# Chunked attention, gated projection and a two-layer block on one core: the first block's order by hand, its transposes and right-hand sums moved

## The chip, the cores and the metric

The kernel runs on one core of a Trainium2 chip. The core has five engines that run at the same time and wait for each other by semaphores: TensorE (PE in the rows; its weight loads are PEld), VectorE (DVE), ScalarE (ACT), GpSimd (POOL) and SyncE (SP), which here only issues transfers. Each works off its own queue in order. The metric is the device time of one execution in microseconds (us); lower is better.

## The reference

Everything is float32 at the interface; the eight sequences of 576 rows and 512 columns make 4,608 rows.

```python
# 1. attention inside chunks of 64 rows, 8 heads of 64 columns
attn = softmax(q_c @ k_c.T / sqrt(64)); x = attn @ v_c          # heads side by side: 512 columns
# 2. gated projection
gate = sigmoid(causal depthwise convolution of x with 5 taps)
y = (gate * (x @ w_val)) @ w_out
# 3. two-layer block with normalised input and residual
yn = (y - mean(y)) / sqrt(var(y) + 1e-6) * g_ln
out = y + relu(yn @ w_ch1) @ w_ch2                              # 512 -> 2048 -> 512
```

The wide weights arrive as pairs of 32-bit words (64-bit floats), which the kernel decodes itself.

## The kernel before, in words

**Number format.** Every float32 matmul is written as three matmuls on a high and a low part: high by high, high by low, low by high. A high part is a rounding copy on ScalarE; the low part is the difference, made on VectorE or GpSimd (`high_low`, L409; `split`, L112).

**Decoding.** A weight tile of 128x512 arrives as raw words (`load_ff`, L141). `decode` (L104) is one ScalarE instruction (L107) and three on VectorE (L108, L109, L110); `split` then adds the high part on ScalarE (L115) and the low part on GpSimd (L116). The decoded first-layer tile is also stored to DRAM (L159) for later use. Of the 32 tiles (16 groups f, one of each layer) those of groups 0 to 3 are made early, those of groups 4 and up just before and during the first block.

**Stages.** Attention and the gated projection run first and leave y in DRAM, nine blocks of 512 rows. Then comes the third part in two forms. The *first block* (rows 0 to 511) is computed directly: for each group f of 128 hidden columns `ff1` (L378) makes 12 matmuls into a hidden tile (psh), ScalarE rectifies it into the high part hh (L387), VectorE makes the low part hl (L388), and `ff2` (L393) multiplies them by the second layer into four accumulators with 12 matmuls (L403). TensorE runs one ff1 ahead of ff2. Two psh buffers alternate.

The other eight blocks go in four passes s of two blocks each, in *paired products* (`ff_pair`, L514): for two groups of hidden columns at once, seven products of 6 matmuls (`prod`, L520) between sums of left-hand weight tiles (wc) and sums of right-hand row tiles (b11, b21, b22 and t1 to t4), accumulated into the two PSUM tiles zy and x; copies and additions (L540, L544) and rectifiers (L535, L536) recover the four hidden tiles h. The second layer of a pair (`ff2_tile`, L487) fills TensorE during the next pair, as the list `fill`.

Around the seam between the two forms stand: the normalisation of the 8 row tiles of pass 0, two at a time (`ln_rows`, L346: statistics L352, L353 and small corrections on VectorE, a square root and the scaling L366 on ScalarE, transposes L369 on TensorE, copies L371 on ScalarE into xt); the right-hand sums (`right_operands`, L453), made from xt by VectorE additions (L463) and high and low parts (L410, L411); the left-hand sums of pair p (`make_pair`, L421), made from stored decoded tiles that are loaded again (raws, L433, L434), with subtractions on VectorE (L435 to L438) and low parts on GpSimd (L411), then stored (L443) for the later passes. Their tiles form a ring; ring positions 0 to 3 use the same memory as the first-layer tiles of groups 0 to 3 and 8 to 11.

**What sets the order.** A scheduler of the framework orders each engine's instructions at build time by priority and by modelled times; on the chip the order is fixed. Inside `manual_schedule` an engine follows the order of the program instead. Before, that holds for TensorE up to unit 7 of attention and from the paired products on, not in the first block. Memory pools that are opened after others are closed (`s_1`, `s_0`) take over their place, and instructions that write there wait for the last reader.

## Time and profile before

| | |
|---|---|
| median of 3 runs | 1196.09 us (1195.82 to 1197.68) |
| the profiled execution | 1193.61 us, its span 1191.8 us |
| TensorE busy | 1114.5 us, 94% of the span; mean granted clock 0.977 |
| VectorE busy | 738.2 us, 62% |
| ScalarE busy | 527.4 us, 44% |
| GpSimd busy | 158.1 us, 13% |

All rows come from the one profiled execution, times counted from its span's start. Attention and the gated projection take the first 378 us. The first block's first hidden product starts at 378.6 us, its last accumulation ends at 493.5 us, and the paired products follow. A row of the timeline is one instruction, or several alike in a run (x12), with its start, its length and in brackets the time the engine was idle before it and who ended the wait. Instructions on TensorE overlap, so twelve that are 0.39 us long each can take 2.96 us in all.

### The profile page before, as it was taken

The numbers are of one execution on the slowest core, as the hardware profiler recorded it, in microseconds if no ns is written. First come the engines' busy times: TensorE is split into PE (matmuls) and PEld (weight loads), VectorE is DVE, ScalarE is ACT, GpSimd is POOL, SyncE is SP. The second block draws the span as 40 slices with busy tenths as digits, with TensorE's granted clock in tenths as the row PEclk, the third lists the DMA queues.
The fourth block names the chain that finished last, engine by engine and source line by source line (L and its number), as shares of the span: only waits on it lengthen the run. The fifth ranks groups of instructions, "written<-read, shape, count | busy, mean of one in ns | idle before, by whom it ended". The sixth has DMA issues, their size and how long they took to land.

```text
span 1191.8 us, 18298 instructions
## 1 busy us (share of the span) xinstructions
PE 1114.5 (94%) x7128; PEld 902.3 (76%) x7128; DVE 738.2 (62%) x1237; ACT 527.4 (44%) x972; POOL 158.1 (13%) x160
## 2 busy tenths in 40 slices
PE   7859999899999688789999999999999999999998
PEld 6747777777777566568888878888788887878876
DVE  6878899988894985644564753534835436442433
ACT  4557678676666564333443323332413424221221
POOL 2221133111211433322221000000000000000000
PEclk8979999999999999989999999999999999999999
DMA  7655676655113673233333353332532332622212
GB/s 182 172 114 131 166 190 182 176 148 131 45 63 126 213 248 119 98 133 124 142 124 106 126 194 105 106 124 89 198 120 89 124 106 98 223 86 89 89 36 79
DMA packets 168860, 155.37 MB, mean 130 GB/s; under 512 B 120622, under 2 KB 128838, under 8 KB 168774
## 3 DMA queue, kind: packets, MB, share of 16 engines
q1 hardware_dynamic: 163590, 144.76, 39.7%
q10 hardware_dynamic: 5184, 9.44, 2.1%
q8 instruction: 56, 0.92, 0.3%
q14 instruction: 30, 0.25, 0.1%
HBM read 116.41 MB, written 37.75 MB: 129 GB/s over the span
## 4 chain that ended last, share of the span: by engine, by line
PE 61%; DVE 26%; ACT 5%; issue 3%; SPq 2%; DMA 1%; POOL 1%; DVEq 0%; POOLq 0%; ACTq 0%
PE acc L501 14%; PE x L526 14%; PE psf L501 14%; PE zy L526 9%; DVE cg L281 8%; PE psv L295 3%; DVE da L109 2%; DVE pr L211 2%; DVE da L110 2%; PE pso L295 2%; DVE sm L208 2%; PE psh L295 2%; DVE ex L202 1%; PE pst L369 1%; DVE mx L199 1%
## 5 line engine op out<-in xcount | busy, mean ns | idle before, releaser
L544 DVE TENSOR_TENSOR c<-x,c 128x512 f32<-128x512 f32 x96 | 66.1, 689 | 231.5 <-ACT c L540 175.1
L501 PE MATMUL acc<-w,h 128*128 128x512 f32 x768 | 186.0, 391 | 0.0
L501 PE MATMUL psf<-w,h 128*128 128x512 f32 x768 | 186.0, 391 | 0.0
L501 PEld LDWEIGHTS acc<-w,h 128*128 128x128 f32 x768 | 144.2, 188 | 31.4
L501 PEld LDWEIGHTS psf<-w,h 128*128 128x128 f32 x768 | 144.2, 188 | 31.3
L526 PE MATMUL x<-t,wc 128*128 128x512 f32 x576 | 149.4, 395 | 4.6 <-DVE c L544 4.2
L540 ACT ACTIVATE c<-zy 128x512 f32<-128x512 f32 x96 | 57.9, 603 | 195.2 <-PE zy L526 195.2
L526 PEld LDWEIGHTS x<-t,wc 128*128 128x128 f32 x576 | 109.3, 190 | 29.6 <-DVE c L544 5.1
L535 ACT ACTIVATE h<-c 128x512 fp32r<-128x512 f32 x96 | 60.5, 631 | 135.8 <-DVE c L544 135.2
L281 DVE SCALAR_TENSOR_TENSOR cg<-xf,cw,cg 128x516 f32<-128x516 f32 (+1 forms) x176 | 116.3, 707 | 0.8 <-ACT cg L279 0.6
L506 DVE TENSOR_TENSOR yt<-psf,yt 128x512 f32<-128x512 f32 x128 | 88.0, 689 | 23.8 <-PE psf L501 19.7
L526 PE MATMUL zy<-b,wc 128*128 128x512 f32 x384 | 100.1, 397 | 0.0
L526 PEld LDWEIGHTS zy<-b,wc 128*128 128x128 f32 x384 | 72.1, 190 | 14.9
L536 DVE SCALAR_TENSOR_TENSOR h<-c,h 128x512 fp32r<-128x512 f32 x96 | 68.0, 709 | 13.1 <-ACT h L535 12.7
L269 POOL TENSOR_TENSOR xl<-xf,xh 128x512 fp32r<-128x512 f32 (+1 forms) x40 | 50.3, 1260 | 154.1 <-ACT xh L268 153.9
L295 PE MATMUL psv<-xh,vh 128*128 128x512 f32 x144 | 60.3, 419 | 7.1 <-DVE gv L309 6.1
L411 POOL TENSOR_TENSOR wc<-raws,wc 128x256 fp32r<-128x256 f32 x56 | 48.4, 885 | 132.5 <-ACT wc L410 132.4
L295 PE MATMUL pso<-oh,gh 128*128 128x512 f32 x144 | 60.1, 417 | 5.6 <-ACT gh L312 5.1
L295 PE MATMUL psv<-xl,vh 128*128 128x512 f32 x144 | 57.5, 399 | 0.9 <-POOL xl L269 0.9
L295 PE MATMUL pso<-oh,gl 128*128 128x512 f32 x144 | 56.9, 397 | 0.7 <-DVE gl L313 0.7
L295 PE MATMUL psv<-xh,vl 128*128 128x512 f32 x144 | 57.4, 398 | 0.0
L526 PE MATMUL zy<-t,wc 128*128 128x512 f32 x192 | 50.6, 399 | 7.0 <-ACT t L410 3.9
(114 smaller groups left out, 1777.7 us busy)
## 6 DMA issues: line engine op xcount, KB each, us to landing
wc<-wc SPq DMA_DIRECT2D x112, 512.0 KB, 3.2
raw<-in_moe_w_ch SPq DMA_DIRECT2D x32, 512.0 KB, 5.0
yr<-yd SPq DMA_DIRECT2D x48, 256.0 KB, 3.0
vr<-in_v SPq DMA_DIRECT2D x144, 64.0 KB, 2.6
yd<-y ACTq DMA_DIRECT2D x36, 256.0 KB, 2.5
kr<-in_k SPq DMA_DIRECT2D x64, 128.0 KB, 2.9
qr<-in_q SPq DMA_DIRECT2D x64, 128.0 KB, 3.0
out<-yt SPq DMA_DIRECT2D x20, 256.0 KB, 3.1
```

The costliest lines, as they stand in the source:

```text
L109: nc.vector.scalar_tensor_tensor(out=au, in0=hw, scalar=0x80000000, in1=au, op0=ALU.bitwise_and, op1=ALU.bitwise_or)
L269: nc.gpsimd.tensor_tensor(out=xl[j][:, :, lo:hi], in0=src, in1=xh[j][:, :, lo:hi], op=ALU.subtract)
L281: nc.vector.scalar_tensor_tensor(out=o, in0=x[:, f, i + lo:i + hi], scalar=cw[:, i * CT + f:i * CT + f + 1], in1=o, op0=ALU.mult, op1=ALU.add,
L295: nc.tensor.matmul(out=ps, lhsT=lt, rhs=rh, start=(i == 0), stop=(i == n - 1))
L411: eng.tensor_tensor(out=lo, in0=a, in1=hi, op=ALU.subtract)
L501: nc.tensor.matmul(out=ps, lhsT=lt, rhs=rh, start=(g == 0 and k == 0 and (first or half)), stop=(g == 1 and k == 2 and (last or half)),)
L506: nc.vector.tensor_tensor(out=yt[i], in0=ps, in1=yt[i], op=ALU.add)
L526: nc.tensor.matmul(out=ps, lhsT=lt, rhs=rh, start=(start and c == 0 and i == 0), stop=(c == 1 and i == 2), skip_group_check=True)
L535: nc.scalar.activation(out=t[:, 0, :], in_=src, func=ACTF.Relu)
L536: nc.vector.scalar_tensor_tensor(out=t[:, 1, :], in0=src, scalar=0.0, in1=t[:, 0, :], op0=ALU.max, op1=ALU.subtract)
L540: nc.scalar.activation(out=t, in_=zy, func=ACTF.Copy)
L544: nc.vector.tensor_tensor(out=t, in0=x, in1=t, op=ALU.add)
```

## The change

In the first block TensorE's order is now written by hand, from the first hidden product on: `manual_schedule` opens before the block instead of behind it. `ln_rows` is split: it only normalises, and `turn_rows` does the transposes and copies. The rows of pair i are loaded ahead, normalised at high priority two groups before they are transposed, and transposed behind the hidden products 3, 5, 7 and 9. The rectifier and the low part of the hidden tile get high priority too. Weights are decoded at the end of each turn of the loop and loaded one group later. The first-layer tiles of groups 8 to 11 move to a pool of their own, and those of groups 12 to 15 take the ring's memory. After group 12's turn the pools are changed over and the right-hand sums are issued, so that they fall into the last three groups. The last second product (ff2 of group 15) and the remaining pools become the one filler of the first pair, behind its first two products, and that pair's first rectifier comes after the filler.

```diff
--- before.py
+++ after.py
@@ -151,7 +151,7 @@
     def split_ff(f, pool):
         r1, r2 = wraw.pop(f)
         g, m = divmod(f, NFA)
-        if g % 2 == 0:
+        if g in (0, 3):
             t = wA.tile([P, 2, DM], F32R, tag=f"s{NFA + m}", name="w0")
         else:
             t = p2[f"w{g}"].tile([P, 2, DM], F32R, tag=f"w{m}", name="w0")
@@ -343,7 +343,7 @@
         nc.sync.dma_start(out=t, in_=rows(s, i)[0])
         return t
 
-    def ln_rows(ys, i):
+    def ln_rows(ys):
 
         n = len(ys)
         mv = p2["b"].tile([P, n, 2], F32, tag="mv", name="mv")
@@ -364,6 +364,11 @@
         nc.vector.scalar_tensor_tensor(out=w, in0=mv[:, :, 0], scalar=-1.0, in1=r, op0=ALU.mult, op1=ALU.mult)
         for t, y in enumerate(ys):
             nc.scalar.activation(out=y, in_=y, func=ACTF.Identity, scale=r[:, t:t + 1], bias=w[:, t:t + 1])
+        return ys
+
+    def turn_rows(ys, i):
+
+        for t, y in enumerate(ys):
             ps = ps_t.tile([P, CT, P], F32, tag="t", name="pst")
             for c in range(CT):
                 nc.tensor.transpose(out=ps[:, c, :], in_=y[:, c * P:(c + 1) * P], identity=ident)
@@ -384,8 +389,9 @@
         chain(ps, ops)
         a = p2["h"].tile([P, BLK], F32R, tag="hh", name="hh")
         b = p2["h"].tile([P, BLK], F32R, tag="hl", name="hl")
-        nc.scalar.activation(out=a, in_=ps, func=ACTF.Relu)
-        nc.vector.scalar_tensor_tensor(out=b, in0=ps, scalar=0.0, in1=a, op0=ALU.max, op1=ALU.subtract)
+        with tc.high_priority():
+            nc.scalar.activation(out=a, in_=ps, func=ACTF.Relu)
+            nc.vector.scalar_tensor_tensor(out=b, in0=ps, scalar=0.0, in1=a, op0=ALU.max, op1=ALU.subtract)
         hh[j, f] = (a, b)
 
     acc = {}
@@ -516,6 +522,7 @@
         zy = ps_d.tile([P, BLK], F32, tag="d", name="zy")
         x = ps_d.tile([P, BLK], F32, tag="d", name="x")
         h = {}
+        first = s == 0 and p == 0
 
         def prod(ps, k, nm, start):
             g = (s * NPR + p) * 7 + k
@@ -551,8 +558,11 @@
         c = copy()
         prod(x, 1, "b11", True)
         add(c)
-        relu((0, 0), c)
+        if not first:
+            relu((0, 0), c)
         run(0, 3)
+        if first:
+            relu((0, 0), c)
         prod(zy, 2, "t1", True)
         d = copy()
         prod(x, 3, "t2", False)
@@ -638,7 +648,7 @@
             yt0 = p2["0"].tile([P, HB, DM], F32, name="yt0")
             y0 = y_dram[0].rearrange("(t p) d -> p t d", p=P)
             nc.sync.dma_start(out=yt0, in_=y0)
-            ln_rows([yt0[:, i, :] for i in range(HB)], 0)
+            turn_rows(ln_rows([yt0[:, i, :] for i in range(HB)]), 0)
             nc.sync.dma_start(out=yt0, in_=y0)
             for i in range(0, HB, 2):
                 ts = slice(i * P, (i + 2) * P)
@@ -676,8 +686,10 @@
     p2["w"] = ctx.enter_context(tc.tile_pool(name="wB", bufs=1, reuse_waits="tile"))
     s_1 = ExitStack()
     p2["w1"] = s_1.enter_context(tc.tile_pool(name="w1p", bufs=1, reuse_waits="tile"))
+    p2["w2"] = s_1.enter_context(tc.tile_pool(name="w2p", bufs=1, reuse_waits="tile"))
     stg2 = s_1.enter_context(tc.tile_pool(name="stg2", bufs=2, reuse_waits="tile"))
-    p2["w3"] = s_1.enter_context(tc.tile_pool(name="w3p", bufs=1, reuse_waits="tile"))
+    order = ExitStack()
+    order.enter_context(tc.manual_schedule(engines={mybir.EngineType.PE}))
 
     def next_ff(f):
         if NFA <= f < NF:
@@ -685,33 +697,43 @@
             load_ff(f, pool)
             split_ff(f, pool)
 
-    def rows_of(s, i, t):
+    def pair_rows(i):
+        t = stg2.tile([P, 2, DM], F32, tag="y", name="yr")
         for k in range(2):
-            nc.sync.dma_start(out=t[:, k, :], in_=rows(s, i + k)[0])
+            nc.sync.dma_start(out=t[:, k, :], in_=rows(0, i + k)[0])
         return [t[:, k, :] for k in range(2)]
 
     next_ff(NFA)
     next_ff(NFA + 1)
+    ys = {0: pair_rows(0)}
     for f in range(NF):
         ff1(0, f)
+        if f in (3, 5, 7, 9):
+            turn_rows(ys.pop(f - 3), f - 3)
         if f > 0:
             ff2(0, f - 1)
-        next_ff(f + NFA + 2)
-        if f in (3, 5, 7, 9):
-            ln_rows(rows_of(0, f - 3, stg2.tile([P, 2, DM], F32, tag="y", name="yr")), f - 3)
-    ff2(0, NF - 1)
-    s_1.close()
-    p2["xb"] = ctx.enter_context(tc.tile_pool(name="xb", bufs=1, reuse_waits="tile"))
-    s_0.close()
-    p2["hr"] = ctx.enter_context(tc.tile_pool(name="p2r", bufs=5, side="right", reuse_waits="tile"))
-    p2["wx"] = ctx.enter_context(tc.tile_pool(name="p2w", bufs=1, side="right", reuse_waits="tile"))
-    p2["c"] = ctx.enter_context(tc.tile_pool(name="pc", bufs=2, reuse_waits="tile"))
-    p2["yt"] = ctx.enter_context(tc.tile_pool(name="pyt", bufs=2, reuse_waits="tile"))
+        if f in (1, 3, 5, 7):
+            if f < 7:
+                ys[f + 1] = pair_rows(f + 1)
+            with tc.high_priority():
+                ln_rows(ys[f - 1])
+        if f > 0:
+            next_ff(f + NFA + 1)
+        if f == NF - 4:
+            s_1.close()
+            p2["xb"] = ctx.enter_context(tc.tile_pool(name="xb", bufs=1, reuse_waits="tile"))
+            p2["c"] = ctx.enter_context(tc.tile_pool(name="pc", bufs=2, reuse_waits="tile"))
+            right_operands()
     make_pair(0)
-    right_operands()
-    order = ExitStack()
-    order.enter_context(tc.manual_schedule(engines={mybir.EngineType.PE}))
-    fill = []
+
+    def open_rest():
+        ff2(0, NF - 1)
+        s_0.close()
+        p2["hr"] = ctx.enter_context(tc.tile_pool(name="p2r", bufs=5, side="right", reuse_waits="tile"))
+        p2["wx"] = ctx.enter_context(tc.tile_pool(name="p2w", bufs=1, side="right", reuse_waits="tile"))
+        p2["yt"] = ctx.enter_context(tc.tile_pool(name="pyt", bufs=2, reuse_waits="tile"))
+
+    fill = [open_rest]
     for s in range(NS):
         for p in range(NPR):
             fill = ff_pair(s, p, fill)
@@ -719,7 +741,7 @@
                 load_yt(s)
             if s + 1 < NS and 2 <= p < 6:
                 i = 2 * (p - 2)
-                ln_rows([load_rows(s + 1, i + k) for k in range(2)], i)
+                turn_rows(ln_rows([load_rows(s + 1, i + k) for k in range(2)]), i)
         if s + 1 < NS:
             right_operands()
     for fn in fill[HB:] + fill[:HB]:

```

The scheduler still orders the other engines, so the change moves more than the diff shows. On TensorE, at the transposes of the first pair of rows, before (yr the rows, pst the transposed tile; w_4933 is group 5's first-layer tile, w_4854 group 3's second-layer tile):

```order
L403 MATMUL acc<-w_4854,hl 128x512
L403 MATMUL acc<-w_4854,hh 128x512 x2
L403 MATMUL acc<-w_4854,hl 128x512
L295 MATMUL psh<-xn_4575,w_4933 128x512
L295 MATMUL psh<-xn_4576,w_4933 128x512
L295 MATMUL psh<-xn_4575,w_4933 128x512
L369 MATMUL pst<-ident,yr 128x128 x4
L295 MATMUL psh<-xn_4575,w_4933 128x512
L369 MATMUL pst<-ident,yr 128x128 x4
```

and of the change (w_4845 is group 3's first-layer tile, w_4801 group 2's second-layer tile):

```order
L295 MATMUL psh<-xn_4576,w_4845 128x512
L295 MATMUL psh<-xn_4575,w_4845 128x512 x2
L295 MATMUL psh<-xn_4576,w_4845 128x512
L295 MATMUL psh<-xn_4575,w_4845 128x512
L374 MATMUL pst<-ident,yr 128x128 x8
L409 MATMUL acc<-w_4801,hh 128x512 x2
L409 MATMUL acc<-w_4801,hl 128x512
```

The eight transposes moved from inside hidden product 5 to the place behind hidden product 3, ahead of second product 2.

On VectorE, at the end of the block, before (hl the low parts of groups 12 to 15, b_ and t_ the low parts of the right-hand sums, xt the additions in place):

```order
L437 TENSOR_TENSOR raws<-raws 128x256
L438 TENSOR_TENSOR raws<-raws 128x256
L388 SCALAR_TENSOR_TENSOR hl<-psh,hh 128x512 x4
L411 TENSOR_TENSOR b_5849<-xt,b_5849 128x1024
L411 TENSOR_TENSOR b_5852<-xt,b_5852 128x1024
L406 TENSOR_TENSOR yt_4577<-acc,yt_4577 128x512 x4
L411 TENSOR_TENSOR b_5855<-xt,b_5855 128x1024
L463 TENSOR_TENSOR xt<-xt 128x2x512
L544 TENSOR_TENSOR c<-x,c 128x512
L463 TENSOR_TENSOR xt<-xt 128x2x512
```

and of the change, from the low part of group 11 on:

```order
L394 SCALAR_TENSOR_TENSOR hl<-psh,hh 128x512
L417 TENSOR_TENSOR b_5704<-xt,b_5704 128x1024
L417 TENSOR_TENSOR b_5707<-xt,b_5707 128x1024
L417 TENSOR_TENSOR b_5710<-xt,b_5710 128x1024
L469 TENSOR_TENSOR xt<-xt 128x2x512
L394 SCALAR_TENSOR_TENSOR hl<-psh,hh 128x512
L469 TENSOR_TENSOR xt<-xt 128x2x512
L417 TENSOR_TENSOR t_5722<-xt,t_5722 128x1024
L469 TENSOR_TENSOR xt<-xt 128x2x512
L417 TENSOR_TENSOR t_5715<-xt,t_5715 128x1024
L469 TENSOR_TENSOR xt<-xt 128x2x512
L394 SCALAR_TENSOR_TENSOR hl<-psh,hh 128x512
```

The right-hand sums moved from behind the last low part to between those of groups 11, 12 and 13.

On TensorE, from the first block into the paired products, before (acc the second products of group 15, zy and x the products of pair 0):

```order
L403 MATMUL acc<-w_5557,hh 128x512 x2
L403 MATMUL acc<-w_5557,hl 128x512
L403 MATMUL acc<-w_5557,hh 128x512 x2
L403 MATMUL acc<-w_5557,hl 128x512
L526 MATMUL zy<-b_5849,wc 128x512 x6
L526 MATMUL x<-b_5852,wc 128x512 x6
L526 MATMUL zy<-t_5860,wc 128x512 x6
L526 MATMUL x<-t_5864,wc 128x512 x6
L526 MATMUL zy<-b_5855,wc 128x512 x6
```

and of the change (w_5579 is group 14's second-layer tile, w_5629 group 15's):

```order
L409 MATMUL acc<-w_5579,hh 128x512 x2
L409 MATMUL acc<-w_5579,hl 128x512
L533 MATMUL zy<-b_5704,wc 128x512 x6
L533 MATMUL x<-b_5707,wc 128x512 x6
L409 MATMUL acc<-w_5629,hh 128x512 x2
L409 MATMUL acc<-w_5629,hl 128x512
L409 MATMUL acc<-w_5629,hh 128x512 x2
L409 MATMUL acc<-w_5629,hl 128x512
L409 MATMUL acc<-w_5629,hh 128x512 x2
L409 MATMUL acc<-w_5629,hl 128x512
L409 MATMUL acc<-w_5629,hh 128x512 x2
L409 MATMUL acc<-w_5629,hl 128x512
```

The first two products of pair 0 moved ahead of the last second product.

## Rows read from the trace of the kernel before

**Rows 1.** Busy time by stretches: PE, PEld, DVE, ACT, POOL, then granted clock, DMA share.

```profile
380.00:460.00 80.00, 64.11 (x273) 50.58 (x271) 73.27 (x127) 45.17 (x95) 39.52 (x30) 0.96 0.62 204
...
493.50:523.40 29.90, 18.36 (x55) 13.03 (x55) 21.48 (x22) 12.52 (x24) 12.36 (x11) 0.77 0.49 175
523.40:1191.80 668.40, 661.46 (x2923) 538.97 (x2921) 318.18 (x533) 205.68 (x402) 29.31 (x38) 1.00 0.34 117
```

**Rows 2.** Timeline of TensorE in the block: start, length, line, operation, idle before.

```profile
392.57 2.96 PE L295 MATMUL psh<-xn,w 128*128 128x512 f32 x12
395.37 0.63 PE L403 MATMUL acc<-w,hh 128*128 128x512 f32 x2
...
413.91 1.11 PE L369 MATMUL pst<-ident,yr 128*128 128x128 f32 x4 [6.04 <-ACT yr L366]
...
415.96 3.76 PE L295 MATMUL psh<-xn,w 128*128 128x512 f32 x8
...
460.98 1.12 PE L369 MATMUL pst<-ident,yr 128*128 128x128 f32 x4 [4.33 <-ACT yr L366]
...
468.48 2.96 PE L295 MATMUL psh<-xn,w 128*128 128x512 f32 x12
```

**Rows 3.** VectorE's groups by form, 380 to 460 us: busy, mean ns, idle before.

```profile
L110 DVE SCALAR_TENSOR_TENSOR da<-raw,da 128x512 uint32<-128x512 uint32 x21 | 22.6, 1083 | 0.1
L109 DVE SCALAR_TENSOR_TENSOR da<-raw,da 128x512 uint32<-128x512 uint32 x21 | 17.9, 856 | 0.2
L108 DVE TENSOR_SCALAR da<-da 128x512 uint32<-128x512 uint32 x21 | 10.3, 488 | 10.4 <-ACT da L107 10.4
```

**Rows 4.** Timeline of VectorE: the first decoding step, the low part of tile 10.

```profile
382.01 0.43 DVE L108 TENSOR_SCALAR da<-da 128x512 uint32<-128x512 uint32 x1 [10.19 <-ACT da L107]
...
459.33 0.68 DVE L388 SCALAR_TENSOR_TENSOR hl<-psh,hh 128x512 fp32r<-128x512 f32 x1
```

**Rows 5.** Timeline of TensorE in the passage.

```profile
493.55 1.52 PE L526 MATMUL zy<-b,wc 128*128 128x512 f32 x6
...
500.32 0.50 PE L526 MATMUL zy<-t,wc 128*128 128x512 f32 x1 [3.89 <-ACT t L410]
503.89 2.50 PE L526 MATMUL zy<-t,wc 128*128 128x512 f32 x5 [3.07 <-DVE t L411]
...
513.98 1.80 PE L526 MATMUL x<-t,wc 128*128 128x512 f32 x6 [3.38 <-DVE c L544]
...
523.41 4.28 PE L501 MATMUL acc<-w,h 128*128 128x512 f32 x18
```

**Rows 6.** Timeline of VectorE in the passage.

```profile
494.49 1.21 DVE L411 TENSOR_TENSOR b<-xt,b 128x1024 fp32r<-128x1024 f32 x1
...
511.67 0.80 DVE L435 TENSOR_TENSOR raws<-raws 128x256 f32<-128x256 f32 x1 [2.74 <-DMA raws<-ad]
```

**Rows 7.** Timeline of TensorE before the block.

```profile
369.07 0.50 PE L295 MATMUL pso<-oh,gh 128*128 128x512 f32 x1 [0.36 <-ACT gh L312]
```

**Rows 8.** Timeline of GpSimd: low parts of left-hand weights.

```profile
467.01 1.44 POOL L411 TENSOR_TENSOR wc<-raws,wc 128x256 fp32r<-128x256 f32 x2 [7.62 <-ACT wc L410]
497.01 9.10 POOL L411 TENSOR_TENSOR wc<-raws,wc 128x256 fp32r<-128x256 f32 x6 [28.56 <-ACT wc L410]
```

**Rows 9.** The page's costliest groups: busy, mean ns, idle before and its end.

```profile
L544 DVE TENSOR_TENSOR c<-x,c 128x512 f32<-128x512 f32 x96 | 66.1, 689 | 231.5 <-ACT c L540 175.1
...
L540 ACT ACTIVATE c<-zy 128x512 f32<-128x512 f32 x96 | 57.9, 603 | 195.2 <-PE zy L526 195.2
```

**Rows 10.** Timeline of SyncE's queue: output stores, loads of raw tiles.

```profile
492.81 2.12 SPq L407 DMA_DIRECT2D out<-yt  x4
...
506.98 0.79 SPq L433 DMA_DIRECT2D raws<-ad  x1
```

**Rows 11.** Instructions of line 110, 380 to 460 us: shortest, median, longest ns.

```profile
L110 DVE SCALAR_TENSOR_TENSOR da<-raw,da x21: 669/685/1786, 383.7 to 455.3; 128x512 uint32<-128x512 uint32 x21
```

**Rows 12.** Instructions of line 388: shortest, median, longest ns.

```profile
L388 DVE SCALAR_TENSOR_TENSOR hl<-psh,hh x16: 676/686/693, 383.1 to 488.9; 128x512 fp32r<-128x512 f32 x16
```

## The prediction

> **What bounds the kernel now.** I read the busy time by stretches first [rows 1]. From 523.4 us to the end TensorE is busy 661.5 of 668.4 us at full clock: what is saved before that point arrives at the end undiminished. The change rewrites the two stretches before it, the first block (380 to 493.5 us) and the passage into the paired products (493.5 to 523.4 us). From 380 to 460 us VectorE is busy 73.3 of 80 us while TensorE is idle for 16; in the passage TensorE works 18.4 of 29.9 us, at a granted clock of 0.77.
>
> Then TensorE's instructions in time. Twelve matmuls of one product take 2.80 us (392.57 to 395.37), 0.233 us each. It waits 6.04 us for normalised rows ahead of a transpose, after which eight matmuls take 3.76 us, 0.47 each, the 1.2 GHz level where 2.4 was granted before the wait; a later transpose costs 4.33 us [rows 2].
>
> Why are the rows late? VectorE's groups say it: the three decoding instructions take 22.6 + 17.9 + 10.3 = 50.8 of its 73.3 us [rows 3]. It begins with them at 382.01 us and starts the low part of hidden tile 10 at 459.33 us [rows 4]; of the 80 us it is idle for 2.0 before that and 4.7 within. So VectorE bounds the first block up to tile 10, and TensorE's waits are its shadow. An order can move the waits; it does not shorten VectorE's list.
>
> In the passage the waits are of another sort: 3.89 and 3.07 us for right-hand sums still being made, and 3.38 us for an addition on VectorE [rows 5], which stood in its queue behind a subtraction that had waited 2.74 us for a transfer [rows 6].
>
> **The change part by part.** *Preparation before the block.* ScalarE now does all normalising and scaling ahead of two gate copies; before, one of them made TensorE wait 0.36 us [rows 7]. I take +0.4 us, between 0 and 1.
>
> *Transposes.* TensorE's order by hand puts the first pair's transposes behind the fourth hidden product; before they lay inside the sixth. From the first decoding step VectorE's new order has 37 instructions up to the last correction of that pair, and one costs 73.27/127 = 0.577 us [rows 1]: 382.0 + 21.3 = 403.3 us, and ScalarE needs 0.8 us more. TensorE is there at 395.4, so it waits some 8.7 us, longer than before, and then runs at half rate for some 6 us. But VectorE does not wait with it. Its next need of TensorE is the low part of tile 4, possible from about 413.6 us (404.1, transposes and second products at half rate to 410, 2.8 us of first products, 0.8 us for the copy), and this stands 18 instructions further, at 413.7 us. The later pairs are normalised two groups ahead and cost nothing; that cover is gone if VectorE falls 11 us behind.
>
> *Decoding behind normalisation.* From the first decoding step to the low part of tile 10 VectorE has the same work before and after (21 weight tiles, 11 low parts, 11 row statistics). So that low part ends at 459.3 + 0.7 = 460.0 us as before, if its idleness stays 4.7 us. Bounds: none, 455.3; twice as much, 464.7. I take 460.0, where the rows have it. Weights are no bound then: the tile for group 9 is decoded some 20 us before its use, and loads issued one group later still have a group to spare.
>
> *What the block gains.* Before, the thirteenth hidden product starts at 468.48 us, since the last transposes (4.33 us of waiting, then half rate) come behind the low part of tile 10 [rows 2]. Now only 11 matmuls lie between: 460.0 + 2.5 = 462.5 us. Gain 6.0 us (1.3 to 10.7).
>
> *Right-hand sums in the last groups.* Seven high and low pairs and four additions on 128x1024 elements, 1.21 us each on VectorE [rows 6], now stand between the low parts of tiles 11 to 14, which are wanted every 5.6 us. Between 12 and 13 lie five of them and a low part, 6.9 us with ScalarE's copies chained in: I charge 1.2 us. Bounds: nothing, if they fit; 3.2 us, if GpSimd's subtractions stretch them. Two of those took 1.44 us alone and six 9.10 us beside these sums [rows 8], 0.80 us more for each; four fall here.
>
> *Left-hand weights.* Groups 12 to 15 now hold the tiles that pair 0's weights need, so GpSimd writes these during the last groups; before, part of them at 467 us [rows 8]. Each tile comes free some 15 us before its use and takes under 2 us: no cost.
>
> *The passage.* Before, 29.86 us (493.55 to 523.41) [rows 5]. Its 54 matmuls at 0.233 us are 12.6 us. What stays: a copy of 0.60 and an addition of 0.69 [rows 9] with three handovers of 0.2 (my estimate), 1.9 us ahead of the third product on x; the second addition, 1.1; the last rectifier, less six matmuls that cover it, 0.5. And one wait that I think is the late one now: the raw tiles of pair 2. Their load stands in SyncE's queue behind stores that wait for GpSimd, which waits until the four output stores have landed, since its tiles lie where the first block's rows were. Counted from the last second product: additions done at 0.9 us, the stores issued by 2.8 (2.12 us for four), landed some 2 us later, four subtractions of 0.72 to 7.7, the load issued at 8.4, and 4.7 us from issue to VectorE (506.98 to 511.67) [rows 6, 10]: 13.1 us. VectorE has two subtractions of these tiles ahead of the rectifier's low part, so x is free at 14.9. TensorE is there at 11.9. I charge 3.0 us, bounds 0 and 6. The passage then takes 12.6 + 6.5 = 19.1 us: gain 10.8 us.
>
> Sum: 6.0 + 10.8 - 0.4 - 1.2 = 15.2 us. The profiled execution took 1193.61 us, the span being 1191.8 of it; it becomes 1178.4. The median of the runs shown lies 2.5 us above it: 1180.9, say 1181.
>
> **A rule weighed.** A decoding step takes 0.669 us at best and 1.786 at worst [rows 11], the low part of a hidden tile 0.676 to 0.693 in all 16 cases [rows 12]; only the first reads both operands from SBUF. The Trainium skill, SBUF — State Buffer, section "SBUF: two separate sides", gives a reason: a VectorE instruction with two SBUF inputs and a GpSimd one need the same port pair, an exclusive lock, and the later one blocks until the other is through. By that rule, the trace agrees. It speaks against the change where pair 0's weights now meet the right-hand sums: seven subtractions of 0.72 us would hold VectorE for 5.0 us, and the sum would be 10.2 us.
>
> **Rivals.** *Covered passage.* If pair 2's raw tiles land in time (3.0), the low parts keep up (1.2) and VectorE loses none of its 4.7 us: 15.2 + 8.9 = 24.1, so 1172. For it: VectorE has little else to do in the passage, and shorter waits leave the clock up. Against: nothing shortens that chain of four waits.
>
> *Contended end.* GpSimd's seven subtractions of 0.72 us [rows 8] each hold VectorE up by their whole length, 5.0 us, low part 13 is late by as much, and the raw tiles cost 5 instead of 3: gain 8.2, so 1188. For it: six took 9.10 us when they met. Against: now they are spread over three groups.
>
> *VectorE and TensorE hold each other (slower).* Both orders are fixed. If VectorE must wait at the low parts of tiles 4 to 11 for products that TensorE could not start, because it stood before a transpose or a low part, its idleness grows; at 4.7 + 15.2 = 19.9 us nothing is gained. Full alternation costs a product of 2.8 and a copy of 0.8 us in each of eight groups, 28.8 us: 13.6 us slower, 1210. For it: the 8.7 us wait at the first transposes. Against: two hidden tiles can be under way at once, and from tile 2 to tile 10 VectorE's work per group, some 8 us, exceeds TensorE's 5.6.
>
> *It does not do what it says.* VectorE reaches tile 10 no earlier than before; if pair 1, which waits for the same stores, takes back what is gained, 1195.
>
> **How the numbers follow.** Chances: forecast 0.58, its own range 1176 to 1186; covered passage 0.20; contended end 0.12; mutual holding 0.06; no change 0.04. The range 1168 to 1190 takes in the first three with their bounds (6.0 may be 10.7; 3.0 may be 0 or 6). About 0.2%, 2.4 us, is what a measurement can tell from no change: faster 0.90, same 0.04, slower 0.06.
>
> **What would show it.** Right: TensorE idle 7 to 10 us before the first transposes, from 395 us on, and nowhere over 4 us later in the block; the low part of tile 10 at 458 to 462 us; no wait for right-hand sums; a passage near 19 us with its longest wait at pair 1's first product on x, behind raw tiles. Wrong: VectorE idle over 10 us between 382 and 460 us; TensorE waiting for GpSimd's weights; the low part of tile 10 well before 455 us, which would mean that VectorE was not the bound.

## The result and the profile after

The changed kernel takes 1179.51 us, median of 4 runs (1179.28 to 1179.55), against 1195.95 us before in the same comparison: ratio 0.986 (95% interval 0.9843 to 0.9877), 16.4 us faster; 1181 was forecast. The profiled execution's span is 1177.7 us against 1191.8. Medians and ratios, here and below, do not count one execution of the changed kernel that took 1815.69 us at a granted clock of 0.556.

Profiled executions differ by up to 6 us before the last gate product on VectorE, where the kernels do all but the same work (it starts at 365.2 to 371.2 us in the fourteen traces of this study). So all stretches below are counted from events inside one trace. From that product (365.53 us before, 367.00 after) to the end it is 826.3 us before and 810.7 after: 15.6 us gained, forecast as 15.2. They fall out thus (the passage runs from pair 0's first product to the end of pair 1's first product on x):

| stretch | before | after | gain | forecast |
|---|---|---|---|---|
| last gate product to first hidden product | 13.07 | 15.02 | -1.95 | -0.4 |
| first hidden product to the 13th | 89.88 | 79.79 | 10.1 | 6.0 |
| 13th to the end of the last second product, pair 0's products not counted | 25.07 | 25.5 | -0.45 | -1.2 |
| passage, the last second product not counted | 29.86 | 21.6 | 8.3 | 10.8 |
| the rest | 668.4 | 668.8 | -0.4 | 0 |

TensorE in the block after the change (start, length, line, operation, idle before it), to be held against [rows 2]:

```profile
382.02 5.76 PE L295 MATMUL psh<-xn,w 128*128 128x512 f32 x24
...
404.89 1.97 PE L374 MATMUL pst<-ident,yr 128*128 128x128 f32 x8 [5.95 <-ACT yr L366]
...
407.51 0.63 PE L409 MATMUL acc<-w,hl 128*128 128x512 f32 x1
...
451.10 0.74 PE L409 MATMUL acc<-w,hh 128*128 128x512 f32 x2 [0.85 <-ACT hh L393]
453.31 0.50 PE L409 MATMUL acc<-w,hl 128*128 128x512 f32 x1 [1.46 <-DVE hl L394]
...
459.40 0.50 PE L409 MATMUL acc<-w,hl 128*128 128x512 f32 x1 [0.26 <-DVE hl L394]
...
461.81 2.96 PE L295 MATMUL psh<-xn,w 128*128 128x512 f32 x12
```

There is one long wait, 5.95 us before the first transposes, and the half rate behind it (407.51: 0.63 us, elsewhere 0.40; the granted clock is 0.50 from 407 to 410.5 us). Then TensorE runs without a wait until 450, and is 0.85, 1.46 and 0.26 us early for hidden tiles 9 and 10. VectorE's two landmarks, and its decoding steps (busy, mean ns, idle before), as [rows 4] and [rows 3]:

```profile
385.43 0.43 DVE L108 TENSOR_SCALAR da<-da 128x512 uint32<-128x512 uint32 x1 [11.87 <-ACT da L107]
...
458.69 0.65 DVE L394 SCALAR_TENSOR_TENSOR hl<-psh,hh 128x512 fp32r<-128x512 f32 x1
```

```profile
L110 DVE SCALAR_TENSOR_TENSOR da<-raw,da 128x512 uint32<-128x512 uint32 x21 | 19.3, 924 | 0.1
L109 DVE SCALAR_TENSOR_TENSOR da<-raw,da 128x512 uint32<-128x512 uint32 x21 | 15.8, 752 | 0.2
L108 DVE TENSOR_SCALAR da<-da 128x512 uint32<-128x512 uint32 x21 | 11.6, 553 | 16.2 <-ACT da L107 15.8
```

From the first decoding step to the low part of tile 10 it is 73.3 us, before 77.3, though the list is the same: the 63 decoding steps take 46.7 us in place of 50.8.

The passage, as [rows 5]; then what SyncE, ScalarE, GpSimd and VectorE do ahead of its longest wait, and the transfers of that stretch (KB each, median us from issue to landing):

```profile
484.58 1.54 PE L533 MATMUL zy<-b,wc 128*128 128x512 f32 x6
...
495.72 1.65 PE L533 MATMUL x<-t,wc 128*128 128x512 f32 x6 [1.41 <-DVE c L551]
498.16 1.65 PE L533 MATMUL x<-t,wc 128*128 128x512 f32 x6 [0.78 <-DVE c L551]
499.65 1.54 PE L533 MATMUL zy<-b,wc 128*128 128x512 f32 x6
506.19 2.93 PE L533 MATMUL x<-b,wc 128*128 128x512 f32 x6 [5.00 <-DVE h L543]
508.92 4.60 PE L507 MATMUL acc<-w,h 128*128 128x512 f32 x18
```

```profile
489.91 2.59 SPq L413 DMA_DIRECT2D out<-yt  x4
...
494.97 1.53 SPq L449 DMA_DIRECT2D wc<-wc  x2
496.55 1.03 SPq L439 DMA_DIRECT2D raws<-ad  x1
497.63 1.01 SPq L440 DMA_DIRECT2D raws<-ad  x1
```

```profile
491.63 0.60 ACT L547 ACTIVATE c<-zy 128x512 f32<-128x512 f32 x1 [3.38 <-PE zy L533]
...
492.64 1.33 ACT L416 ACTIVATE wc<-raws 128x256 fp32r<-128x256 f32 x4
```

```profile
493.13 3.02 POOL L417 TENSOR_TENSOR wc<-raws,wc 128x256 fp32r<-128x256 f32 x4 [3.66 <-ACT wc L416]
```

```profile
503.86 0.81 DVE L441 TENSOR_TENSOR raws<-raws 128x256 f32<-128x256 f32 x1 [4.36 <-DMA raws<-ad]
504.70 0.83 DVE L442 TENSOR_TENSOR raws<-raws 128x256 f32<-128x256 f32 x1
505.46 0.68 DVE L543 SCALAR_TENSOR_TENSOR h<-x,h 128x512 fp32r<-128x512 f32 x1
```

```profile
yt<-yd SPq DMA_DIRECT2D x4, 256.0 KB, 4.7
raws<-ad SPq DMA_DIRECT2D x2, 256.0 KB, 6.3
```

No wait is for right-hand sums any more. Pair 1's first product on x (506.19) waits 5.00 us, for the rectifier's low part at 505.46, which stands behind two subtractions of raw tiles that had waited 4.36 us for their load. That load went out at 496.55 to 498.6, behind stores of pair 1's weights that waited for GpSimd's subtractions (to 496.2); these follow high parts that ScalarE made at 492.64, queued behind its copy of zy. It then took 6.3 us to land, just behind four loads of y rows, and VectorE had it 7.3 us after the first issue; before the change that took 4.7 [rows 6, 10].

### The profile page after: what moved, and what is told of

Read it like the earlier page. It is cut to its first block, busy times and chain, and to the rows that moved or that the text cites. A ratio compares the mean times of both kernels' runs of the same rounds, so it can differ in the third digit from the quotient of the medians.

```text
span 1177.7 us, 18293 instructions
## 1 busy us (share of the span) xinstructions
PE 1112.4 (94%) x7128; PEld 902.3 (77%) x7128; DVE 731.0 (62%) x1237; ACT 526.3 (45%) x972; POOL 159.8 (14%) x160
## 4 chain that ended last, share of the span: by engine, by line
PE 60%; DVE 27%; ACT 6%; issue 3%; DMA 3%; SPq 1%; POOL 1%; DVEq 0%; ACTq 0%; POOLq 0%
PE acc L507 14%; PE x L533 14%; PE psf L507 13%; PE zy L533 9%; DVE cg L281 8%; PE psv L295 3%; DVE pr L211 2%; PE pso L295 2%; DVE sm L208 2%; DVE da L109 2%; DVE da L110 2%; DVE ex L202 1%; DVE gl L313 1%; DVE mx L199 1%; DVE h L543 1%
## 5 line engine op out<-in xcount | busy, mean ns | idle before, releaser
L533 PE MATMUL x<-t,wc 128*128 128x512 f32 x576 | 146.9, 391 | 2.2 <-DVE c L551 2.2
L533 PEld LDWEIGHTS zy<-b,wc 128*128 128x128 f32 x384 | 71.3, 188 | 14.5
L543 DVE SCALAR_TENSOR_TENSOR h<-c,h 128x512 fp32r<-128x512 f32 x96 | 67.7, 705 | 15.6 <-ACT h L542 15.2
L116 POOL TENSOR_TENSOR w<-da,w 128x512 fp32r<-128x512 f32 x32 | 46.9, 1474 | 95.9 <-ACT w L115 95.9
L533 PE MATMUL x<-b,wc 128*128 128x512 f32 x192 | 52.6, 410 | 6.6 <-DVE h L543 5.9
```

The lines of the kernel that those rows point to most:

```text
L116: nc.gpsimd.tensor_tensor(out=lo, in0=a, in1=hi, op=ALU.subtract)
L533: nc.tensor.matmul(out=ps, lhsT=lt, rhs=rh, start=(start and c == 0 and i == 0), stop=(c == 1 and i == 2), skip_group_check=True)
L543: nc.vector.scalar_tensor_tensor(out=t[:, 1, :], in0=src, scalar=0.0, in1=t[:, 0, :], op0=ALU.max, op1=ALU.subtract)
```

## The experiments

All are timed against the kernel before on the same chip in five rounds. The last three columns are from the traces: the block is the first to the 13th hidden product, the passage as above; "VectorE" is first decoding step to the start of the low part of tile 10. In the rows of some kernels the line numbers are a few higher.

| kernel | median us | ratio (95%) | VectorE | block | passage |
|---|---|---|---|---|---|
| before | | 1 | 77.3 | 89.9 | 29.9 |
| changed | 1179.51 | 0.9860 (0.9843, 0.9877) | 73.3 | 79.8 | 21.6 |
| after_again | 1178.93 | 0.9863 (0.9838, 0.9888) | 73.5 | 80.0 | 19.7 |
| e1_sums_after | 1174.63 | 0.9825 (0.9798, 0.9852) | 73.9 | 80.5 | 17.5 |
| e6_sums_behind | 1187.56 | 0.9934 (0.9911, 0.9957) | 73.3 | 79.9 | 29.1 |
| e2_no_gpsimd_low | 1173.25 | 0.9815 (0.9789, 0.9841) | 68.4 | 74.6 | 21.0 |
| e3_turn_later | 1178.69 | 0.9859 (0.9834, 0.9884) | 71.9 | 78.5 | 21.8 |
| e4_relu_first | 1175.58 | 0.9831 (0.9807, 0.9856) | 73.0 | 79.5 | 15.4 |
| e5_prep_by_row | 1176.95 | 0.9845 (0.9819, 0.9870) | 72.9 | 80.6 | 20.9 |
| c2_relu_prep_turn | 1172.91 | 0.9819 (0.9791, 0.9848) | 71.8 | 78.4 | 15.4 |
| e7_before_late_pair | 1190.07 | 0.9936 (0.9913, 0.9959) | 74.5 | 86.1 | 31.0 |
| e8_low_on_vector | 1171.59 | 0.9784 (0.9760, 0.9808) | 63.9 | 72.5 | 19.1 |
| c4_two_pairs | 1171.36 | 0.9789 (0.9764, 0.9814) | 72.8 | 79.4 | 15.4 |
| c5_two_pairs_ff2_first | 1171.87 | 0.9797 (0.9772, 0.9821) | 71.3 | 77.8 | 16.2 |

**The changed kernel again** (after_again). 

> The changed kernel itself once more, so that the others of this group have a run of it on the same chip. Every theory: 1177.5 to 1181.5 us; the block from its first product to the first product of group 12 79.8 us, pair 0's first product to the end of pair 1's first product on x 24.3 us.

Its block is the same to 0.3 us; its passage is 1.9 us shorter, with a wait of 3.91 us where 5.00 stood and the product behind it in 2.07 us where it took 2.93. Pair 2's raw tiles come to VectorE 12.7 us after the last second product, in place of 13.8: between these two executions of one kernel that moves by a microsecond.

**Right-hand sums: e1_sums_after, e6_sums_behind.** The first moves the call behind the block:

```diff
-            right_operands()                  # in the loop, at f == NF - 4
-    fill = [open_rest]
+    open_rest()                               # the last second product
+    right_operands()
+    fill = []
```

> The changed kernel, with its right-hand sums back behind the last second product of the first block, all else as changed. Theory (the passage gained because the sums left it): TensorE waits again for sums in the making, some 3.9 and 3.1 us, and the passage from pair 0's first product to the end of pair 1's first product on x grows from 21.6 us to about 29.9, as before the change: 8.3 us slower than the changed kernel, some 1188 us. Rival (pair 2's raw tiles set the end of the passage, whatever the sums do: they came 13.8 us after the last second product): the sums are nearly free, at most 2 us slower, some 1181 us.

```profile
464.33 3.50 DVE L417 TENSOR_TENSOR b<-xt,b 128x1024 fp32r<-128x1024 f32 x3 [0.26 <-ACT b L416]
...
501.76 0.82 DVE L441 TENSOR_TENSOR raws<-raws 128x256 f32<-128x256 f32 x1 [1.53 <-DMA raws<-ad]
```

Both were wrong, because the edit did not do what was meant: the scheduler put the sums on VectorE where they had been, at 464 to 479 us. What changed was TensorE's order, with the last second product ahead of pair 0. Counted from the 13th hidden product, pair 2's raw tiles come to VectorE 2.0 us earlier (at 501.76 us); from the issue of their load it takes 5.5 us in place of 7.3. Why the load is quicker is not shown; that it meets fewer others on its way would fit. The wait before pair 1's first product on x is 1.29 us, at the price of a wait of 0.51 us for a copy. The second experiment holds the sums back by force:

```diff
+    with ExitStack() as late:
+        for ins in tail:                      # hidden tile 15's copy and low part
+            late.enter_context(tc.issue_after(ins))
         right_operands()
```

(`issue_after` queues what follows on an engine behind that instruction, without a wait for its end.)

> As the first experiment, in which the last second product of the first block stands ahead of pair 0's products and VectorE had made the right-hand sums in the last groups all the same; here ScalarE and VectorE are made to take the sums up only behind the copy and the low part of hidden tile 15. Theory (the passage gained because the sums left it): TensorE waits for sums in the making again, and the stretch from the end of the last second product to the end of pair 1's first product on x, 17.5 us in the first experiment, grows to about 28 to 30: 1183 to 1188 us. Rival (what stretched the sums before the change was GpSimd's subtractions for pair 0, which are now done earlier; alone they take 11 times 1.21 us): 20 to 22 us for that stretch, 1176 to 1180 us.

TensorE of that kernel, then VectorE and GpSimd while the sums are made:

```profile
492.59 0.79 PE L534 MATMUL zy<-t,wc 128*128 128x512 f32 x1 [4.52 <-ACT t L417]
494.87 2.50 PE L534 MATMUL zy<-t,wc 128*128 128x512 f32 x5 [1.49 <-DVE t L418]
...
511.55 2.93 PE L534 MATMUL x<-b,wc 128*128 128x512 f32 x6 [4.23 <-DVE h L544]
```

```profile
491.33 1.22 DVE L418 TENSOR_TENSOR t<-xt,t 128x1024 fp32r<-128x1024 f32 x1
...
493.60 1.22 DVE L418 TENSOR_TENSOR t<-xt,t 128x1024 fp32r<-128x1024 f32 x1
```

```profile
488.60 13.93 POOL L418 TENSOR_TENSOR wc<-raws,wc 128x256 fp32r<-128x256 f32 x6 [3.32 <-ACT wc L417]
```

The waits are back, 4.52 and 1.49 us, and the stretch is 29.1 us against 17.5: the theory holds. Of the 11.6 us between them 6.0 are these waits and 2.9 the longer wait for raw tiles before pair 1 (4.23 against 1.29); the rest is mostly products at half rate. Beside it, VectorE's 128x1024 low parts run at 1.22 us while GpSimd's six subtractions take 13.93 us; before the change VectorE's took 1.74 and GpSimd's six 9.10 [rows 8].

**The first transposes a group later: e3_turn_later.**

```diff
-        if f in (3, 5, 7, 9):
-            turn_rows(ys.pop(f - 3), f - 3)
+        if f in (4, 5, 7, 9):
+            i = 0 if f == 4 else f - 3
+            turn_rows(ys.pop(i), i)
```

> The changed kernel, with the first pair's transposes one group later, behind the fifth hidden product in place of the fourth. Theory (VectorE bounds the block): TensorE's wait of 5.95 us before them falls to at most 1, but comes back ahead of the low parts of tiles 4 to 10, which stand in VectorE's list as late as before; the first product of group 12 starts within 1.5 us of 79.8 us after the block's start, and the time stays, 1177.5 to 1180 us. Rival (TensorE's own list bounds the block from the first transposes on, since it did not wait from 404.9 to 450.1 us): the 5.95 us and most of the 2.7 us at the lower clock behind it are gained: 1171 to 1173.5 us.

```profile
407.54 1.36 PE L374 MATMUL pst<-ident,yr 128*128 128x128 f32 x8 [0.39 <-ACT yr L366]
...
439.26 0.50 PE L409 MATMUL acc<-w,hl 128*128 128x512 f32 x1 [2.42 <-DVE hl L394]
...
454.02 0.50 PE L409 MATMUL acc<-w,hl 128*128 128x512 f32 x1 [0.92 <-DVE hl L394]
```

The 5.95 us are gone (0.39), and 2.42 and 0.92 us come back before low parts, with smaller ones at transposes. The block gains 1.3 us, and the time is that of the changed kernel: VectorE bounds the block, as the forecast had it.

**Without GpSimd's subtractions: e2_no_gpsimd_low, e8_low_on_vector.** For the weights of hidden tiles 4 to 15, 24 of them, the low part (L116) is written by another engine (the two expectations say 8 to 15, but the edits take in all groups from 4 on):

```diff
-        nc.gpsimd.tensor_tensor(out=lo, in0=a, in1=hi, op=ALU.subtract)
+        nc.scalar.activation(out=lo, in_=a, func=ACTF.Copy)               # e2
+        nc.vector.tensor_tensor(out=lo, in0=a, in1=hi, op=ALU.subtract)   # e8
```

> The changed kernel, but for the weights of hidden tiles 8 to 15 GpSimd makes no low parts: ScalarE writes a second copy of the whole weight in their place (that part of the result is another one). ScalarE gets 16 more instructions of 0.62 us, 10 us in all, in the block. Theory (VectorE bounds the block up to hidden tile 10, and GpSimd's subtractions stretch its decoding steps): the 21 steps of line 110 fall from a mean of 924 ns to about 690, those of line 109 from 752 to about 690, those of line 108 from 553 to about 420, some 9 us less, and the 128x2 steps that took 1.2 us fall to 0.15, some 5 us less; TensorE's wait before the first transposes (5.95 us) shrinks below 2 and its waits for the low parts of tiles 9 and 10 (0.85, 1.46, 0.26 us) go: 6 to 10 us faster than the changed kernel, 1170 to 1174 us. Rival (the steps are stretched by something else, or TensorE's own order bounds the block, which ran without a wait from 404.9 to 450.1 us): durations as they were, or shorter without the time following; within 2 us of the changed kernel.

```profile
L110 DVE SCALAR_TENSOR_TENSOR da<-raw,da 128x512 uint32<-128x512 uint32 x21 | 14.2, 685 | 0.1
L109 DVE SCALAR_TENSOR_TENSOR da<-raw,da 128x512 uint32<-128x512 uint32 x21 | 14.2, 682 | 0.1
L108 DVE TENSOR_SCALAR da<-da 128x512 uint32<-128x512 uint32 x21 | 8.6, 419 | 16.7 <-ACT da L107 16.7
```

Every decoding step is at its shortest, and TensorE runs without a wait from the first transposes on; the time, 1173.25 us, is in the range of the theory. The block is only 5.2 us shorter, since 5.3 us of waiting stay ahead of the first transposes, where less than 2 were expected: ScalarE, which makes 24 further copies (15.3 us, not 10), delivers their scaled rows at 402 to 404 us.

> The changed kernel, with the low parts of the weights of hidden tiles 8 to 15 subtracted on VectorE in place of GpSimd. Theory (a GpSimd subtraction holds VectorE's steps for about as long as VectorE would need to do it itself: in the changed kernel 22 of them stretch its list by some 9 us in the decoding steps and 6 in the 128x2 steps, 0.7 us each, against 0.61 us net for one on VectorE): VectorE's list to the low part of tile 10 stays as long or becomes up to 3 us shorter, 70 to 74 us in place of 73.3, and the time is 1176 to 1180 us. Rival (GpSimd takes real work off VectorE, and the stretching is only where both happen to meet): 22 subtractions of 0.69 us come on top, less what is not stretched in the decoding steps, so 4 us or more longer: 1183 us or more.

```profile
L116 DVE TENSOR_TENSOR w<-da,w 128x512 fp32r<-128x512 f32 x24 | 16.1, 684 | 8.3 <-ACT w L115 8.3
L110 DVE SCALAR_TENSOR_TENSOR da<-raw,da 128x512 uint32<-128x512 uint32 x21 | 14.2, 684 | 0.0
L109 DVE SCALAR_TENSOR_TENSOR da<-raw,da 128x512 uint32<-128x512 uint32 x21 | 14.2, 686 | 0.1
...
L108 DVE TENSOR_SCALAR da<-da 128x512 uint32<-128x512 uint32 x21 | 8.9, 424 | 3.5 <-ACT da L107 3.5
```

```profile
403.10 1.36 PE L375 MATMUL pst<-ident,yr 128*128 128x128 f32 x8 [2.93 <-ACT yr L367]
```

The rival is out, and the theory has the direction but not the size: with these low parts on VectorE its list takes 63.9 us, where 70 to 74 were expected, and the time is 1171.59, below its 1176 to 1180. The list is 9.4 us shorter than in the changed kernel, the block 7.3 us, and TensorE's only wait in it is 2.93 us before the first transposes. This one edit beats the changed kernel by 0.8% (intervals 0.9760 to 0.9808 and 0.9838 to 0.9888).

**Pair 0's weights late in the kernel before: e7_before_late_pair.**

```diff
+    with ExitStack() as late:
+        for ins in tail:                      # hidden tile 11's copy and low part
+            late.enter_context(tc.issue_after(ins))
         make_pair(0)
```

> The kernel before, with nothing changed but that ScalarE and VectorE take up pair 0's raw tiles only behind hidden tile 11's copy and low part; so GpSimd writes pair 0's left-hand weights behind the low part of tile 10, as in the changed kernel, and not six of them between 450 and 459 us. Theory (the changed kernel's 4.1 us from the first decoding step to the low part of tile 10 come from these six subtractions, which no longer stretch VectorE's steps): that stretch, 77.3 us before the change, falls by the stretching and by the four subtractions on raw tiles that move behind it, 5 to 7 us in all, to 70.5 to 72.5 us; first product to first product of group 12 falls from 89.9 to 83 to 86 us, and the whole to 1189 to 1192 us. Rival (the order of decoding and normalisation did it): the stretch falls by the 2 to 3 us of the moved subtractions at most, to 74.5 us or more, and the time stays within 2 us of the kernel before, 1193 us or more.

```profile
387.32 0.43 DVE L108 TENSOR_SCALAR da<-da 128x512 uint32<-128x512 uint32 x1 [10.21 <-ACT da L107]
...
461.86 0.69 DVE L388 SCALAR_TENSOR_TENSOR hl<-psh,hh 128x512 fp32r<-128x512 f32 x1
```

74.5 us, not 70.5 to 72.5: 2.8 us gained, half of what the theory asked for and at the edge of what its rival allows; neither holds alone. The median is where the theory had it, 6.4 us below the kernel before in the same comparison; the trace shows less, 2.8 us from the last gate product to the end, with a block 3.8 us shorter and a passage 1.1 us longer. The traced execution was the slowest of seven (1196.05 us, the fastest 1185.74), so how far it stands for the median is not shown.

**Pair 0's last rectifier first: e4_relu_first.** In `make_pair`, for pair 2:

```diff
+        with ExitStack() as late:
+            if p == 2:
+                for ins in rect:              # pair 0's h(1,0): copy and low part
+                    late.enter_context(tc.issue_after(ins))
             make_weights(p)
```

> The changed kernel, with the work on pair 2's raw tiles queued behind pair 0's last rectifier on ScalarE and VectorE; before, that rectifier stood behind it on both. Theory (TensorE's wait of 5.00 us before pair 1's first product on x is the queue order and nothing else): x is free some 1.4 us after pair 0's last product, under pair 1's product on zy, and the wait goes with the 1.4 us that this product loses at the lower clock: 5 to 6.5 us faster than the changed kernel, 1173 to 1174.5 us. Rival (the raw tiles themselves are late: their transfer lands 13 us after the last second product, and pair 1's additions or pair 2's weights wait for them next): the wait moves by some 5 to 7 us of products and comes back at pair 1's second product on zy or at pair 2; at most 2 us gained, 1177.5 us or more.

```profile
501.75 1.66 PE L542 MATMUL x<-b,wc 128*128 128x512 f32 x6
...
516.72 1.66 PE L542 MATMUL x<-t,wc 128*128 128x512 f32 x6 [0.94 <-DVE c L562]
```

The 5.00 us are gone (501.75 follows its forerunner at once) and the passage is 15.4 us. 0.94 us come back at pair 1's third product on x, whose addition stands behind pair 3's raw tiles. The queue order was the wait. The gain is 4.8 to 5.8 us from the last gate product to the end (804.9 against 809.7 and 810.7); the median, 1175.58 us, lies between the theory's 1173 to 1174.5 and the rival's 1177.5.

**The preparation row by row: e5_prep_by_row.** In the preparation, `ln_rows` turns each row tile as soon as it is scaled, as before the change:

```diff
             nc.scalar.activation(out=y, in_=y, func=ACTF.Identity, scale=r[:, t:t + 1], bias=w[:, t:t + 1])
+            if turn:
+                turn_rows([y], t)
```

> The changed kernel, but in the preparation each row tile is normalised and turned in one step, as before the change, so that ScalarE reaches the two gate copies earlier. Theory (the copies stand behind all normalising and scaling, which makes TensorE wait 1.29 and 0.34 us and then run 4 us of products at the lower clock): from the start of the last gate product on VectorE to the block's first product 13.1 us as before the change, in place of 15.0; VectorE's first decoding step moves by the same, so 1.9 us of the whole are gained, 1176 to 1179 us. Rival (the block's end hangs on transfers and VectorE's list, not on when it starts): the 1.9 us come back as waits in the block, and the time stays within 0.5 us.

The last gate product starts at 367.63 us and the first hidden product at 380.73: 13.10 us, the 1.9 are back. From the gate product to the end it gains 0.4 to 1.4 us (809.3 against 810.7 and 809.7), since in the block its products run at half rate for 3 us (granted clock 0.53 from 452 to 455.5 us) behind waits of 1.28 and 1.48 us, which 0.85 and 1.46 did not bring about in the changed kernel. The median gained 2.0 against after_again; intervals of 0.5% cannot tell the two apart. The theory's place is right, its gain partly lost again.

**Together: c2_relu_prep_turn, c4_two_pairs, c5_two_pairs_ff2_first.** Edits of e3, e4 and e5; then e4's for pair 3 behind pair 1's rectifier as well; then also the last second product first.

> The changed kernel with three edits together: pair 2's raw tiles queued behind pair 0's last rectifier, each row tile normalised and turned in one step in the preparation, and the first pair's transposes one group later. Theory (each takes away a wait of its own, and the gains add): 5.2 us in the passage and behind it, 1.9 in the preparation, 1.3 in the block: 8.4 us faster than the changed kernel of this group, some 1171 us. Rival (an earlier block meets the same transfers, so that pair 2's raw tiles come no earlier): only some 5 us, 1174 us or more.

> The three edits together, and also pair 3's raw tiles queued behind pair 1's last rectifier. Theory (the wait of 2.25 us before pair 1's third product on x in the three edits' kernel is the addition queued behind pair 3's raw tiles): it goes, TensorE has no wait left from pair 1's first product on, and the time is 1170 to 1171.5 us, some 8.5 to 9 us faster than the changed kernel. Rival (pair 3's weights then come too late, or pair 3's transfers): a wait of 2 us or more at pair 2 or 3, 1173 us or more.

> As the kernel before in this group, with the last second product of the first block ahead of pair 0's products in place of between them. Theory (nothing in the passage waits for the output stores any more, so their coming 2.8 us earlier buys nothing, and pair 0's copy of zy loses its cover): 0.5 us slower than without it, for the wait of 0.51 us that the first experiment showed. Rival (stores, pair 1's weights and pair 2's raw tiles still set the pace): 1 to 2 us faster.

The three together gain 6.0 us by the medians and 6.9 to 7.9 from the last gate product to the end (802.8 against 809.7 and 810.7), 8.4 being expected; 1172.91 us lies between theory and rival. 2.25 us of waiting have come up before pair 1's third product on x, and the fourth edit removes them: in c4 the only wait of TensorE above 0.2 us from pair 1's first product on is one of 0.78 us, in pair 2, and the median is the theory's. c4 and c5 are equal (802.2 and 802.3 us from the last gate product to the end), so the order of the last second product, which was worth 3 to 4 us in e1 (806.5 against 810.7 and 809.7), is worth nothing once the rectifier goes first. The edit of e8 was not tried with these; what they give together stays open.

## Why the prediction was right

**The mechanism of the block's gain was right.** Before, the 13th hidden product starts 9.15 us after the low part of tile 10 [rows 2, 4], now 3.12 us: 6.0 us, as worked out. e3 confirms that VectorE is the bound: a wait of 5.95 us was moved, and the end hardly stirred.

**The step that failed: "An order can move the waits; it does not shorten VectorE's list."** That put the low part of tile 10 at 460.0 us; counted from the first decoding step, it came 4.1 us sooner. The first pair's last correction shows it too: it comes 18.6 us after the first decoding step, not 21.3, so that TensorE waits 5.95 us before the first transposes and not 8.7. Where nothing holds it, the list advances by 0.60 us for a 128x512 instruction, 0.33 for line 108, 0.34 for a 128x256 and 0.08 for a 128x2 one (starts in e2 and e8). With that the 77.3 and 73.3 us divide as follows, the stretching being what is left:

| kernel | unhindered list | idle | stretching | GpSimd instructions in it |
|---|---|---|---|---|
| before | 49.0 | 4.3 | 24.1 | 29 |
| changed | 49.3 | 4.8 | 19.2 | 22 |
| e7 | 47.8 | 5.2 | 21.6 | 23 |
| e2 (no GpSimd) | 46.0 | 20.4 | 2.0 | 0 |
| e8 (no GpSimd) | 59.4 | 3.2 | 1.3 | 0 |

The 1.3 to 2.0 us that stay without GpSimd show the error of this division. In e8 the list itself is 10.1 us longer than in the changed kernel, with 18 of the 24 subtractions on VectorE before tile 10, and 17.8 us of stretching are gone. One meeting in the changed kernel, GpSimd's subtraction and the decoding step that VectorE took up beside it:

```profile
393.41 1.46 POOL L116 TENSOR_TENSOR w<-da,w 128x512 fp32r<-128x512 f32 x1 [2.50 <-ACT w L115]
```

```profile
393.76 1.67 DVE L110 SCALAR_TENSOR_TENSOR da<-raw,da 128x512 uint32<-128x512 uint32 x1
```

The step takes 1.67 us in place of 0.68 and ends 0.56 us after the subtraction.

So a quarter to a third of VectorE's time there is stretching by GpSimd, 0.83 to 0.94 us for each of its instructions, and an order that moves seven of them out of the way shortens the list. I had taken rows with 0.67 to 1.79 us for one step [rows 11], and their mean, as a fixed price. e7 moved six of the seven in the kernel before and saved 2.5 us of stretching where the change saved 4.9. That leaves 2.4 us to how the remaining 22 meet VectorE's steps in the new order. Taken one by one, against their median in e2 and e8, 26 instructions of VectorE are stretched by more than 0.1 us before, 21 in e7 and 19 after the change (21.7, 18.9 and 15.8 us); what the changed kernel has less than e7 lies mostly in the small corrections on 128x2 elements (5.5 us against 8.3). Why the new order spares these stays open.

The Trainium skill, SBUF — State Buffer, section "SBUF: two separate sides", says that a VectorE instruction in a 2-port mode, or with two SBUF inputs when GpSimd reads SBUF too, and a GpSimd one take a shared port pair as an exclusive lock, and that whoever starts first keeps the other out. The traces agree: without GpSimd lines 109 and 110 fall to 682 and 685 ns, line 108 from 553 to 419, while the low parts hl, which read PSUM, took 678 ns with it and 686 without. Line 108 has one input only, so the rule covers it by a 2-port mode alone, which no run shows. The other half of the rule shows in e6, where GpSimd is the one kept out (2.3 us each, 0.72 alone [rows 8]).

**"Left-hand weights: no cost"** holds, and undersold it: leaving VectorE's bound stretch was a gain.

**Right-hand sums in the last groups** were charged 1.2 us and cost 0.45 at most; the one wait is 0.23 us. The contended end (5.0 us) did not come: the sums lie before the passage, where e6 shows them worth 11.6 us.

**The passage** was forecast at 19.1 us and took 21.6. Its two additions cost 1.41 and 0.78 us (charged 1.9 and 1.1) and the last rectifier nothing (0.5). The wait for pair 2's raw tiles is the late one, at the place named, but 5.00 us in place of 3.0, and the product behind it ran at half rate, 1.4 us that I had not counted. VectorE got the tiles 13.8 us after the last second product, forecast 13.1, but not for the reasons given: ScalarE wrote pair 1's weights at 492.64 us, when the last output store had just been issued, so they did not wait for the stores to land; the load went out 1.9 us earlier than I had reckoned and took 2.6 us longer. Then two subtractions took 0.8 us each in place of 0.43, beside GpSimd, and TensorE was there 0.8 us sooner than thought.

**The preparation** cost 1.95 us, outside its bounds of 0 to 1: waits of 1.29 and 0.34 us for the gate copies and then products of 0.43 us in place of 0.23.

```profile
371.48 0.50 PE L295 MATMUL pso<-oh,gh 128*128 128x512 f32 x1 [1.29 <-ACT gh L312]
...
373.01 0.78 PE L295 MATMUL pso<-oh,gl 128*128 128x512 f32 x1 [0.34 <-DVE gl L313]
373.59 0.63 PE L295 MATMUL pso<-oh,gh 128*128 128x512 f32 x1
```

I had counted ScalarE's work and not the lower clock behind a wait. Misses of +4.8 (block and sums), -2.5 (passage), -1.6 (preparation) and -0.4 (the rest) nearly cancelled: that the sum came within 0.4 us of the 15.6 measured is luck, its terms were further off.

## What to carry to other kernels

Before handing a saturated VectorE's subtraction to GpSimd, look at what VectorE's own steps cost beside it: here a GpSimd subtraction, mostly 1.3 to 1.75 us long, held VectorE for 0.8 to 0.9 us on average, and doing it on VectorE took 0.6. When a wait ends with an instruction that was ready long before, look at what stands ahead of it in its queue; putting pair 0's rectifier ahead of a late transfer took away all 5 us, and no transfer had to be faster. And moving code does not move instructions where a scheduler places them: that e1 had left the sums where they were showed in its trace alone.

## What the runs showed that I had not expected

Stretching reaches very small instructions too. A correction on 128x2 elements of the changed kernel (VectorE), which takes 0.15 us otherwise:

```profile
417.36 1.27 DVE L363 TENSOR_TENSOR r<-r,w 128x2 f32<-128x2 f32 x1
...
419.15 0.15 DVE L364 SCALAR_TENSOR_TENSOR w<-mv,r 128x2 f32<-128x2 f32 x1
```

And the same wait does not always cost the clock: after 1.29 and 0.34 us of waiting in the preparation the products ran at half rate for some 3 us in the changed kernel (granted clock 0.50 from 373.6 to 376.4 us), while in e3, with the same two waits, it stayed at 1.00 (377.2 to 381.0 us) and the stretch from the last gate product to the first hidden product was 13.5 us in place of 15.0.
